# The first half of a gated feed-forward block: second-pair weight operands ahead of the second weight's, a gelu behind a copy, and another order of loads at the half's end

## The chip, the cores and the metric

The kernel runs on one core of a Trainium2 chip. The metric is device time in microseconds (us) of one execution. A core has five engines with an instruction queue each, and each queue is worked in order. TensorE (PE in the profile; PEld is its weight load) multiplies matrices into PSUM. VectorE (DVE) and ScalarE (ACT) work elementwise on PSUM and on-chip memory, GpSimd (POOL) elementwise on on-chip memory alone here. SyncE (SP) issues the DMA transfers. An instruction that waits for another engine's result holds up everything behind it on its own queue.

## The reference, cut to what matters

For 2048 tokens with 576 features, all in float32:

```
xn  = layernorm(x)
s   = linear attention of xn over 32 heads, times wo
h   = gelu_tanh(xn @ w1 + b1)          # w1: 576 x 4608
g   = silu(h @ w2 + b2)                # w2: 4608 x 576
out = x + s * g
```

## The kernel before

**Precision.** Each float32 operand is kept as two parts, a rounded high part and the rest (tiles named `_h` and `_l`, or one tile with both). A product is three matmuls: high by high, high by low, low by high. ACT makes the high part by a cast (line 811 for w1, 754 for w2 and h), DVE the low part by a subtraction (816 and 757). Both read the raw tile, and the low part waits for the high one.

**Stages.** The first 282.6 us make the attention part, and the layernormed x. Then the feed-forward runs over the tokens in two halves of 1024, and in each half over nine *chunks* of 512 of the 4608 hidden features, 18 chunks in all. This text counts them 0 to 17.

**Seven products for eight.** Each matrix product of a chunk is a 2 by 2 block product done with seven block products and sums of blocks (Winograd's variant of Strassen's scheme). A chunk has two *pairs* of feature blocks. For each pair the class `Up` does products M1, M2, M6, M5, M7, M3, M4, in this order, seven matmuls of 512 columns each. M1, M6 and M7 add up in the PSUM tile `a`, M5 and M3 in `e`; M2 and M4 go to the two halves of `bc`. So M6 may start only when ACT has copied M1 out of `a` (line 1107), M7 only when ACT has copied `a` again (`u1_sb`, line 1114), and M3 only when `e` has been copied (`m5_sb`, line 1117). DVE adds these copies to later products (lines 1110, 1120, 1125, 1129), and ACT takes four gelus of the sums (1098). A prime marks the second pair here: M5' is its product 5.

Then the *down product* multiplies the gelus by w2: `product` at line 1233, again seven block products in the order 1, 2, 7, 4, 5, 3, 6, each in two parts of twelve matmuls of 288 columns. Products 2, 4 and 3 add onto the PSUM tiles of 1, 7 and 5, after DVE has added what stood there to the sums `macc` (1239, 1243).

**Operands.** M1 and M2 take the w1 tile `wa`, M6 `w6`, M5 and M4 `wd`, M7 and M3 `wc`. In the first half the kernel makes these tiles itself: POOL makes the differences in place in the raw tile (`T`, lines 800 to 807), then ACT and DVE split them (`hi`, `lo`). They also go to DRAM, and the second half loads them from there. The same is done with w2's seven operands (`W2`, POOL line 1151). The first pair's w1 tiles are made during the chunk before (table `P0`), the second pair's during the first pair's products (table `P1`), w2's about the same time (table `PW2`).

**What sets the order.** Each of these tasks has a step number in a table. A chunk has 28 steps: 0 to 6 stand behind the first pair's products, 7 to 13 behind the second pair's, 14 to 27 behind the halves of the down product's parts. `at_step` writes out what is due after that product's own instructions. DVE, ACT, POOL and PE keep exactly the order in which the code writes instructions.

**The change of halves.** During chunk 8 the other half's x operands are loaded (`load_x_part`, line 1396, and `rxm` by `load_rests`): `h0`, `l0`, `h1`, `l1`, `s1`, `s2`, `s4` and `rxm` with 1 MB each, and three small pieces. Each goes over a tile of the first half, so it can start only after that tile's last product in chunk 8. `X_AT` holds their steps. Three finished output blocks (`C22`, `C21`, `C12`, parts of `macc`) get their silu (line 1309) in chunk 9, and are stored; later parts of the down product write over them.

Of the kernel before, what the change touches and what calls it, by code (L numbers as in the profile page):

```python
# [44 lines left out]
def linear_attention_gated_ffn(ctx, tc, x, xT, wqkv, wo, w1, w1e, b1, w2, b2, out):  # L45
# [733 lines left out]
    class W1:  # L779
# [11 lines left out]

        def T(self, i):

# [130 lines left out]
    def load_rests(half):  # L924

        if not rx:
            rx.append(xp.tile([P, KT, 512], F32R, tag="xh1", name="rxm"))
        t = rx[0]
        load_rest(half, REST_AT[1], 4, t[:, :4].rearrange("p k c -> p (k c)"))
        return {i: t[:, REST_AT[i] - REST_AT[1]] for i in (1, 7, 5, 3)}  # L930
# [25 lines left out]
    def beside(i, k):  # L956
# [14 lines left out]
        else:  # L971
# [24 lines left out]
            if i == 17:  # L996
                w = w1t[0]
                w.hi("a"), w.lo("a")
                for j in (5, 6, 7, 4):
                    w.T(j)  # L1000
                w.hi(6), w.lo(6)
# [9 lines left out]
    for i in range(1, NT + 4):  # L1011
        if 1 < i < NT:
            query(i)
        if i in X_STORES:
            at, src = X_STORES[i]
# [47 lines left out]
    C11, C12, C21, C22, U1 = range(5)  # L1063
# [8 lines left out]
    class Up:  # L1072
# [28 lines left out]
        def step(self, i):  # L1101
            A, E, Z = self.a, self.e, self.z[:, 0, :]
            B, C = self.bc[:, 0, :], self.bc[:, 1, :]
            tt = nc.vector.tensor_tensor
            if i == 1:
                self.mm(A, 1)
                nc.scalar.copy(m1_sb, A)  # L1107
            elif i == 2:
                self.mm(B, 2)
                tt(B, B, m1_sb, op=ADD)  # L1110
                self.gelu(0, 0, B)
            elif i == 6:
                self.mm(A, 6, first=False)
                nc.scalar.copy(u1_sb, A)
            elif i == 5:
                self.mm(E, 5)
                nc.scalar.copy(m5_sb, E)
            elif i == 7:
                self.mm(A, 7, first=False)
                tt(Z, A, m5_sb, op=ADD)  # L1120
                nc.scalar.copy(u2_sb, A)  # L1121
                self.gelu(1, 1, Z)
            elif i == 4:
                self.mm(C, 4)
                tt(C, C, u2_sb, op=ADD)
                self.gelu(0, 1, C)
            else:
                self.mm(E, 3, first=False)
                tt(E, E, u1_sb, op=ADD)  # L1129
                self.gelu(1, 0, E)  # L1130


    class W2:
# [9 lines left out]

        def T(self, i):
            src = self.src
# [26 lines left out]
    class HOps:  # L1172
# [6 lines left out]
        def add(self, pr, g):  # L1179
            for (par, b), t in g.items():  # L1180
                self.A[pr, b, par] = t
                self.src[{(0, 0): 1, (0, 1): 2, (1, 1): 4, (1, 0): "-"}[b, par], pr] = t
# [204 lines left out]
        "s2": (16, x_hi, 2, 6), "s1": (20, x_lo, 0, None), "h1": (8, x_hi, 3, 4),  # L1387
        "l1": (12, x_lo, 3, None),
    }
    X_AT = {"h0": 8, "l0": 11, "s2": 11, "h1": 13, "l1": 13, "s1": 13, "s4": 14}  # L1390
    x_new = {}

    def load_x_part(k):
# [10 lines left out]

    def plan_w1(add, w, base, T, hi, lo):
        for table, what in ((T, w.T), (hi, w.hi), (lo, w.lo)):
            for i, at in table.items():
                add(base + at, what, i)

    P1 = dict(  # L1410
        T={5: 1, 6: 1, 7: 3, 4: 3},
        hi={"a": 0, 6: 4, "c": 7, "d": 7},
        lo={"a": 0, 6: 5, "c": 8, "d": 8},
    )
    P0 = dict(
        T={5: 18, 6: 18, 7: 19, 4: 19},
        hi={"a": 16, 6: 23, "c": 25, "d": 27},
        lo={"a": 17, 6: 24, "c": 26, "d": 28},
# [1 line left out]


    PW2 = dict(
        T={5: -1, 7: 2, 6: 2, 4: 4},
        hi={1: -2, 3: -1, 2: 0, 5: 2, 7: 5, 6: 6, 4: 9},
        lo={1: -1, 3: 0, 2: 1, 5: 3, 7: 6, 6: 7, 4: 10},
    )

    def plan_w2(n, ahead):
        for what in ("hi", "lo", "T"):
# [7 lines left out]
        hi={  # L1437
            (1, 0): 7, (2, 0): 9, (7, 0): 10, (1, 1): 11, (2, 1): 12, (7, 1): 15, (4, 0): 16,
            (4, 1): 17, (5, 1): 18, (5, 0): 19, (6, 0): 20, (3, 0): 21, (3, 1): 22, (6, 1): 23,
        },  # L1440
        lo={
            (1, 0): 10, (2, 0): 10, (7, 0): 11, (1, 1): 12, (2, 1): 13, (7, 1): 15, (4, 0): 16,
            (4, 1): 17, (5, 1): 18, (5, 0): 19, (6, 0): 20, (3, 0): 21, (3, 1): 22, (6, 1): 23,
        },
# [17 lines left out]
    s2, s1, s4 = z.tiles  # L1462
# [4 lines left out]
    for step in range(n_chunks):  # L1467
        half, c = divmod(step, NC)
        base = step * NS
        plain = step == n_chunks - 1  # L1470
        h = HOps(c)
        if half == 0:
            plan_w1(add, w1t[2 * step + 1], base, **P1)
            if step == 0:
                plan_w2(0, True)
            plan_w2(step, False)
        change = step == NC - 1
        if not plain:
            add(base + (11 if change else 7), load_we, 2 * step + 2)
            add(base + (16 if change else 14), load_we, 2 * step + 3)  # L1480
        if half == 0 and c < NC - 1:
            add(base + 0, make, W1, w1t, 2 * step + 2)
            add(base + 4, make, W1, w1t, 2 * step + 3)
            add(base + 1, lambda n=2 * step + 2, base=base: plan_w1(add, w1t[n], base, **P0))
            make(W2, w2t, step + 1)
            add(base + 16, w2t[step + 1].load_raw)
            plan_w2(step + 1, True)
        elif not plain:
            add(base + (11 if change else 7), make, W1Loaded, w1t, 2 * step + 2)
            add(base + (11 if change else 14), load_six, 2 * step + 2)  # L1490
            add(base + (16 if change else 14), make, W1Loaded, w1t, 2 * step + 3)
            if step + 2 < n_chunks:
                make(W2, w2t, step + 1)
                for i, at in W2_NEXT.items():
                    add(base + at + 10 * change, lambda i=i, n=step + 1: w2t[n].load(i))
            else:
                make(W2, w2t, step + 1)

                w = w2t[step + 1]
                add(base + 7, w.load_raw)  # L1500
                for f in range(CF):
                    add(base + 22 + f, lambda f=f, w=w: (w.plain(f), w.hi(("p", f))))
                    add(base + 24 + f, w.lo, ("p", f))
        if not plain:
            if half == 0 and c == NC - 1:
                for k, at in X_AT.items():
                    add(base + at, load_x_part, k)
                add(base + 14, lambda: x_new.update(rs=load_rests(0)))
                add(base + 25, silu_first, C11)
                for k in range(2):  # L1510
                    add(base + 26 + k, combine, C12, nc.vector, slice(2 * k, 2 * k + 2))
                    add(base + 26 + k, combine, C21, nc.gpsimd, slice(2 * k, 2 * k + 2))
            for what in ("S", "hi", "lo"):
                for (i, pr), at in PH[what].items():
                    add(base + at, getattr(h, what), i, pr)
        if half == 1 and c == 0:
            add(base, combine, C22, nc.vector, slice(0, 2))
            add(base + 1, combine, C22, nc.vector, slice(2, 4))
            for m in (C22, C21, C12):
                add(base + 13, silu_first, m)  # L1520
        if half == 1 and c:
            for k in range(2):
                tiles = {}
                def load(k=k, t=7 + c, tiles=tiles):
                    tiles[0] = finish_tiles(k)
                    finish_load(t, k, tiles[0])
                add(base, load)
                add(base + 4, lambda k=k, t=7 + c, tiles=tiles: finish(t, k, tiles[0]))
        if plain:
            for m in (C12, C21, C22):  # L1530
                add(base + 4, combine, m, nc.gpsimd)
            for t, at in enumerate((6, 7, 12, 13, 5, 12, 12, 12)):
                add(base + at, load_xs, t)
            for b, f, at, lo in (
                (0, 0, 7, 8), (0, 1, 8, 9), (1, 0, 10, 10), (1, 1, 10, 11), (0, 2, 11, 12),
                (0, 3, 12, 13), (1, 3, 13, 13), (1, 2, 13, 13),
            ):
                add(base + at, tail_split, b, f)
                add(base + lo, tail_lo, b, f)
        for j in range(CF // 2):  # L1540
            n = 2 * step + j
            u = Up(n, w1t.pop(n), xs)
            for k, i in enumerate(UP):
                u.step(i)
                h.add(j, u.g)
                at_step(base + 7 * j + k)
        if plain:
            break
        held = {}
        for k, i in enumerate(ORDER):  # L1550
            for q2 in (0, 2):
                product(c, i, q2, [h.ops[i, 0], h.ops[i, 1]], w2t[step].ops[i], held)
                at_step(base + 14 + 2 * k + q2 // 2)
        if half == 0 and c == NC - 1:
            xs = x_operands(*(x_new[k] for k in ("h0", "l0", "h1", "l1", "s1", "s2", "s4", "rs")))
# [50 lines left out]
```

## Time and profile before

| what | value |
|---|---|
| time, median of 3 runs | 1113.93 us (1113.92 to 1115.60) |
| the profiled execution's own time | 1114.99 us |
| its span | 1113.3 us |
| DMA, mean over the span | 218 GB/s |
| chunks 0 to 8 | 282.61 to 700.48 us |
| chunks 9 to 17 | 700.48 to about 1105 us |

The page's first part gives each engine's busy time. The view of waits sums for an engine the idle time that ended when another engine's instruction was done: us in total, times, longest. The timeline has the start and length of each instruction. The view by stretches gives each stretch's length and what each engine was busy in it. Matmuls overlap, so a group's clean pitch is the time from one start to the next.

### The profile page before, as it was taken

Reading aid. Unit: us, or ns where it says so; the run is one execution under the profiler, and the core shown is the slowest. Engines: PE = TensorE matmul, PEld = TensorE weight load, DVE = VectorE, ACT = ScalarE, POOL = GpSimd, SP = SyncE. Lnnn points to the kernel's source line nnn. Section 1 sums busy time; section 2 is a strip of 40 time slices with the busy share of each in tenths; the row PEclk is TensorE's granted clock in tenths of the full one; section 3 lists DMA queues with packets and bytes.
Section 4 is the critical chain, followed back from the end, with each engine's and each line's share of the span. In section 5 each row is a group of like instructions: output and inputs, shape, how many; then the busy total and the mean of one; then the engine's idle time right before and its main releaser. Section 6 shows DMA issues by size and latency. Waiting matters only on the chain.

```text
span 1113.3 us, 18079 instructions
## 1 busy us (share of the span) xinstructions
PE 1095.2 (98%) x6702; PEld 1007.4 (90%) x6702; DVE 773.9 (70%) x1096; ACT 547.8 (49%) x954; POOL 455.7 (41%) x394
## 2 busy tenths in 40 slices
PE   9999999999999999999999999999999999999998
PEld 8999989999798888988889889898998998989988
DVE  7655338888688887888878888565474664754756
ACT  6444455454646455464554645445344253353552
POOL 3443214232647555475554754315133233241340
PEclk9999999999999999999999999999999999999999
DMA  6755124675759467485674829988667667766452
GB/s 212 216 137 143 58 76 161 205 255 178 272 238 331 188 226 257 186 327 191 224 260 187 324 114 377 379 310 280 215 221 229 221 219 235 221 221 209 146 187 87
DMA packets 84224, 242.78 MB, mean 218 GB/s; under 512 B 11430, under 2 KB 23718, under 8 KB 81448
## 3 DMA queue, kind: packets, MB, share of 16 engines
q1 hardware_dynamic: 84136, 241.62, 63.3%
q8 instruction: 53, 0.87, 0.3%
q14 instruction: 35, 0.29, 0.1%
HBM read 145.66 MB, written 93.99 MB: 215 GB/s over the span
## 4 chain that ended last, share of the span: by engine, by line
PE 87%; ACT 4%; DVE 3%; DMA 3%; issue 2%; SPq 0%; POOL 0%; ACTq 0%; DVEq 0%; POOLq 0%
PE pm L1233 32%; PE a L1090 11%; PE e L1090 8%; PE bc L1090 7%; PE pk L320 6%; PE pq L320 5%; PE ps_s L730 5%; PE pv L320 4%; PE pd L1349 2%; DMA rxm<-rq_dram 1%; PE ps_kva L381 1%; DVE wc L816 1%; DMA we<-op 1%; PE ptp L712 1%; DVE wd L816 1%
## 5 line engine op out<-in xcount | busy, mean ns | idle before, releaser
L1239 DVE TENSOR_TENSOR macc<-pm,macc 128x576 f32<-128x576 f32 x218 | 164.7, 756 | 63.4 <-PE pm L1233 61.4
L754 ACT CAST h_h<-g 128x512 fp32r<-128x512 f32 x204 | 121.8, 621 | 139.1 <-PE pm L1233 138.6
L757 DVE TENSOR_TENSOR h_l<-g,h_h 128x512 fp32r<-128x512 f32 x204 | 158.5, 780 | 12.1 <-ACT h_h L754 11.4
L1151 POOL TENSOR_TENSOR w2raw<-w2raw 128x576 f32<-128x576 f32 x36 | 60.7, 1687 | 99.6 <-DVE w__5651 L757 11.5
L1199 POOL TENSOR_TENSOR mid<-g 128x512 f32<-128x512 f32 x34 | 45.7, 1345 | 116.1 <-ACT g L1098 116.1
L1098 ACT ACTIVATE g<-bc,b1c 128x512 f32<-128x512 f32 x72 | 49.6, 689 | 54.7 <-DVE bc L1110 41.2
L1107 ACT COPY mid<-a 128x512 f32<-128x512 f32 x36 | 21.2, 588 | 96.9 <-PE a L1090 96.0
L1193 POOL TENSOR_TENSOR g<-g 128x512 f32<-128x512 f32 x34 | 51.9, 1526 | 31.1 <-DVE h_l L757 29.8
L1120 DVE TENSOR_TENSOR z<-a,mid 128x512 f32<-128x512 f32 x36 | 25.2, 700 | 56.4 <-PE a L1090 56.4
L1321 POOL TENSOR_TENSOR fin1l<-fin1h,fin1l 128x288 f32<-128x288 f32 x8 | 6.7, 837 | 120.7 <-DMA fin1l<-s_dram 69.9
L1110 DVE TENSOR_TENSOR bc<-bc,mid 128x512 f32<-128x512 f32 x36 | 25.0, 693 | 42.6 <-PE bc L1090 40.7
L1196 POOL TENSOR_TENSOR g<-g 128x512 f32<-128x512 f32 x34 | 49.2, 1448 | 7.6 <-DVE h_l L757 5.5
L1190 POOL TENSOR_TENSOR g<-g 128x512 f32<-128x512 f32 x34 | 47.5, 1397 | 2.7
L1121 ACT COPY mid<-a 128x512 f32<-128x512 f32 x36 | 21.1, 587 | 52.8 <-DVE z L1120 52.8
L695 POOL TENSOR_TENSOR pbuf<-phiq,den 128x576 f32<-128x576 f32 x16 | 19.4, 1212 | 63.6 <-DVE den L694 63.6
L320 PE MATMUL pk<-wkv_h,xh 128*128 128x288 f32 (+1 forms) x160 | 38.2, 321 | 0.4 <-ACT xh L247 0.4
L339 DVE SCALAR_TENSOR_TENSOR phik<-pk,ek 128x576 f32<-128x576 f32 x16 | 12.1, 758 | 38.2 <-ACT ek L337 38.2
L320 PE MATMUL pk<-wkv_l,xh 128*128 128x288 f32 (+1 forms) x160 | 38.2, 321 | 0.0
L1090 PE MATMUL e<-s,wd 128*128 128x512 f32 x108 | 30.0, 400 | 7.8 <-DVE wd L816 7.8
L1129 DVE TENSOR_TENSOR e<-e,mid 128x512 f32<-128x512 f32 x36 | 25.1, 696 | 16.8 <-PE e L1090 16.8
L730 PE MATMUL ps_s<-kw_h,th 128*128 128x288 f32 x160 | 35.5, 303 | 0.0
L320 PE MATMUL pq<-wq_h,xh 128*128 128x288 f32 x160 | 34.8, 299 | 0.0
(894 smaller groups left out, 3638.6 us busy)
## 6 DMA issues: line engine op xcount, KB each, us to landing
we<-we_dram SPq DMA_DIRECT2D x36, 448.0 KB
w2raw<-w SPq DMA_DIRECT2D x10, 1152.0 KB
w1raw<-w SPq DMA_DIRECT2D x18, 512.0 KB
op_a<-wa SPq DMA_DIRECT2D x18, 512.0 KB
op_c<-wc SPq DMA_DIRECT2D x18, 512.0 KB
op_d<-wd SPq DMA_DIRECT2D x18, 512.0 KB
wc<-op_c SPq DMA_DIRECT2D x18, 512.0 KB
wa<-op_a SPq DMA_DIRECT2D x18, 512.0 KB
```

The source lines that it names most:

```text
L320: nc.tensor.matmul(ps[:, h, : ws.stop - ws.start], st, w[:, k, ws], start=(begin and i == 0), stop=(end and i == len(seq) - 1), skip_group ...
L730: nc.tensor.matmul(ps[:, h, :HD], st[:, k, :], w[:, k, h * HD : (h + 1) * HD], start=(i == 0), stop=(i == len(seq) - 1),)
L754: nc.scalar.copy(pair[0], src)
L757: eng.tensor_tensor(pair[1], src, pair[0].bitcast(F32), op=SUB)
L1090: nc.tensor.matmul(ps, st, mv, start=first and n == 0, stop=n == len(seq) - 1, skip_group_check=True,)
L1098: nc.scalar.activation(g, ps, AF.Gelu_apprx_tanh, bias=b1c[:, f : f + 1])
L1151: tt(dst, a, b, op=SUB)
L1190: tt(src[5, pr], A(1, 0), A(1, 1), op=ADD)
L1193: tt(src[6, pr], src[5, pr], A(0, 0), op=SUB)
L1196: tt(src[3, pr], A(0, 1), src[6, pr], op=SUB)
L1233: nc.tensor.matmul(ps[:, q, :HD], hs[p][st][:, cs], m[:, p, :], start=(n == 0 and i not in CHAIN), stop=(n == 5), skip_group_check=True,)
L1239: nc.vector.tensor_tensor(dst, src, dst, op=ADD)
```

## The change

- In the first half's chunks the tasks of the tables move. The second pair's `wc` and `wd` are made at steps 5 and 6 in place of 7 and 8, and POOL's two sums for them at step 2 in place of 3. w2's operands for products 7, 6 and 4 come one or two steps later, the low parts for 3 and 2 and POOL's sums for 7 and 6 one step later.
- In `Up`, for all chunks, the gelu of M2's sum is written after the copy of `a` behind M6, and no longer ahead of it.
- At the change of halves the loads of x come in another order and at other steps; `load_rests` (`rxm`) goes from step 14 to 12.
- The three silus of chunk 9 are due at steps 13, 15 and 18; before, all were due at step 13.

```diff
@@ Up.step
             elif i == 2:
                 self.mm(B, 2)
                 tt(B, B, m1_sb, op=ADD)
-                self.gelu(0, 0, B)
             elif i == 6:
                 self.mm(A, 6, first=False)
                 nc.scalar.copy(u1_sb, A)
+                self.gelu(0, 0, B)
@@ loads of x
-    X_AT = {"h0": 8, "l0": 11, "s2": 11, "h1": 13, "l1": 13, "s1": 13, "s4": 14}
+    X_AT = {"l0": 8, "s2": 8, "h0": 9, "s1": 12, "h1": 13, "l1": 13, "s4": 14}
...
-                add(base + 14, lambda: x_new.update(rs=load_rests(0)))
+                add(base + 12, lambda: x_new.update(rs=load_rests(0)))
@@ P1
-        T={5: 1, 6: 1, 7: 3, 4: 3},
-        hi={"a": 0, 6: 4, "c": 7, "d": 7},
-        lo={"a": 0, 6: 5, "c": 8, "d": 8},
+        T={5: 1, 6: 1, 7: 2, 4: 2},
+        hi={"a": 0, 6: 4, "c": 5, "d": 5},
+        lo={"a": 0, 6: 5, "c": 6, "d": 6},
@@ PW2
-        hi={1: -2, 3: -1, 2: 0, 5: 2, 7: 5, 6: 6, 4: 9},
+        hi={1: -2, 3: -1, 2: 0, 5: 2, 7: 6, 6: 8, 4: 10},
...
@@ silus
-            for m in (C22, C21, C12):
-                add(base + 13, silu_first, m)
+            for m, at in ((C22, 13), (C21, 15), (C12, 18)):
+                add(base + at, silu_first, m)
```

The instruction order on DVE in chunk 3, from its second pair's `wa` on, stood as follows. Here `bc6`, `z6` and `e6` are the first pair's sums and `bc7` the second's; `wc_7` and `wd_7` are the second pair's w1 tiles; the tiles `w2_3` are w2's, of which this queue makes the low parts.

```order
L816 TENSOR_TENSOR wa_7_4711<-w1raw7_4287,wa_7_4711 128x512
L757 TENSOR_TENSOR w2_3__4688<-w2raw3_4483,w2_3__4688 128x576
L1110 TENSOR_TENSOR bc6_4698<-bc6_4698,mid_3217 128x512
L757 TENSOR_TENSOR w2_3__4716<-w2raw3_4483,w2_3__4716 128x576
...
L816 TENSOR_TENSOR w6_7_4775<-w1t6_4734,w6_7_4775 128x256
L1125 TENSOR_TENSOR bc6_4698<-bc6_4698,mid_3217 128x512
L757 TENSOR_TENSOR w2_3__4793<-w2raw3_4483,w2_3__4793 128x576
L757 TENSOR_TENSOR w2_3__4805<-w2raw3_4483,w2_3__4805 128x576
L1110 TENSOR_TENSOR bc7_4812<-bc7_4812,mid_3217 128x512
L816 TENSOR_TENSOR wc_7_4822<-w1raw7_4287,wc_7_4822 128x512
L816 TENSOR_TENSOR wd_7_4824<-w1raw7_4287,wd_7_4824 128x512
L757 TENSOR_TENSOR w2_3__4860<-w2raw3_4483,w2_3__4860 128x576
```

In the changed kernel it is this:

```order
L816 TENSOR_TENSOR wa_7_4711<-w1raw7_4287,wa_7_4711 128x512
L1110 TENSOR_TENSOR bc6_4698<-bc6_4698,mid_3217 128x512
L757 TENSOR_TENSOR w2_3__4688<-w2raw3_4483,w2_3__4688 128x576
...
L816 TENSOR_TENSOR w6_7_4775<-w1t6_4729,w6_7_4775 128x256
L1125 TENSOR_TENSOR bc6_4698<-bc6_4698,mid_3217 128x512
L816 TENSOR_TENSOR wc_7_4790<-w1raw7_4287,wc_7_4790 128x512
L816 TENSOR_TENSOR wd_7_4792<-w1raw7_4287,wd_7_4792 128x512
L757 TENSOR_TENSOR w2_3__4813<-w2raw3_4483,w2_3__4813 128x576
L1110 TENSOR_TENSOR bc7_4817<-bc7_4817,mid_3217 128x512
L757 TENSOR_TENSOR w2_3__4844<-w2raw3_4483,w2_3__4844 128x576
...
L1120 TENSOR_TENSOR z7_4818<-a7_4815,mid_3217 128x512
```

The low parts of `wc_7` and `wd_7` moved ahead of two w2 tiles and of the second pair's first sum; the last w2 tile went behind `z7`.

On ACT at the start of chunk 3, before, behind the copy of M1 (`a6` is the first pair's tile `a`, `e6` its `e`):

```order
L754 CAST w2_3__4716<-w2raw3_4483 128x576
L1098 ACTIVATE g_4731<-bc6_4698,b1c_78 128x512
L1114 COPY mid_3217<-a6_4696 128x512
L754 CAST w2_3__4747<-w2raw3_4483 128x576
L1117 COPY mid_3217<-e6_4697 128x512
```

In the changed kernel:

```order
L754 CAST w2_3__4716<-w2raw3_4483 128x576
L1113 COPY mid_3217<-a6_4696 128x512
L1098 ACTIVATE g_4742<-bc6_4698,b1c_78 128x512
L754 CAST w2_3__4746<-w2raw3_4483 128x576
L1117 COPY mid_3217<-e6_4697 128x512
```

The copy of `a` and the gelu changed places. Where ACT must load a function table for the gelu, in chunks 0, 9 and 10, that load now stands between the copy and the gelu.

On SP in chunk 8, the loads at the change of halves, before (`l0r` to `s4r` are the x tiles; `we`, `wa` and `wd` are w1's for chunk 9):

```order
L1396 DMA l0r<-x_dram 128x2048
L751 DMA op_c<-wc_7263 128x1024
L751 DMA op_d<-wd_7265 128x1024
L1396 DMA h0r<-x_dram 128x2048
...
L1396 DMA s2r<-x_dram 128x2048
L920 DMA s2r<-rq_dram 128x512
L1396 DMA h1r<-x_dram 128x2048
L920 DMA h1r<-rq_dram 128x512
L1396 DMA l1r<-x_dram 128x2048
L1396 DMA s1r<-x_dram 128x2048
L1396 DMA s4r<-x_dram 128x2048
L920 DMA rxm<-rq_dram 128x2048
```

In the changed kernel:

```order
L751 DMA op_d<-wd_7235 128x1024
L1396 DMA l0r<-x_dram 128x2048
L1396 DMA s2r<-x_dram 128x2048
L920 DMA s2r<-rq_dram 128x512
L1396 DMA h0r<-x_dram 128x2048
...
L1396 DMA s1r<-x_dram 128x2048
L920 DMA rxm<-rq_dram 128x2048
L1396 DMA h1r<-x_dram 128x2048
L920 DMA h1r<-rq_dram 128x512
L1396 DMA l1r<-x_dram 128x2048
L1396 DMA s4r<-x_dram 128x2048
```

The load of `rxm` went from the last place to before `h1r`, `l1r` and `s4r`, and `s2r` went ahead of `h0r`.

More of the change, by code (lines that the diff above doesn't have):

```diff
@@ L1422, in linear_attention_gated_ffn @@
     PW2 = dict(
-        T={5: -1, 7: 2, 6: 2, 4: 4},
-        hi={1: -2, 3: -1, 2: 0, 5: 2, 7: 5, 6: 6, 4: 9},
-        lo={1: -1, 3: 0, 2: 1, 5: 3, 7: 6, 6: 7, 4: 10},
+        T={5: -1, 7: 3, 6: 3, 4: 4},
+        hi={1: -2, 3: -1, 2: 0, 5: 2, 7: 6, 6: 8, 4: 10},
+        lo={1: -1, 3: 1, 2: 2, 5: 3, 7: 7, 6: 9, 4: 11},
     )
```

## The prediction

> **What bounds the kernel now.** I read the page's busy times first, then the engines' waits, the stretches, and the timeline of one chunk. The page:
>
> ```profile
> PE 1095.2 (98%) x6702; PEld 1007.4 (90%) x6702; DVE 773.9 (70%) x1096; ACT 547.8 (49%) x954; POOL 455.7 (41%) x394
> ```
>
> PE works nearly all the time, so only its pauses can be won. The waits of its weight loads and matmuls name them:
>
> ```profile
> PEld e L1090 <- DVE wd L816: 11.6, 9, 2.2
> PEld a L1090 <- ACT mid L1114: 4.8, 9, 1.1
> PE a L1090 <- DMA rxm<-rq_dram: 1.1, 1, 1.1
> PE pm L1233 <- ACT h_h L754: 0.5, 1, 0.5
> PE pm L1233 <- DVE h_l L757: 0.4, 1, 0.4
> ```
>
> Two waits come once in each of the nine first-half chunks: for the low part of `wd`, and for the copy of `a`. What a chunk loses is in the stretches of chunks 0, 3, 8, 9 and 10 (length, then busy times, granted clock, DMA share, GB/s):
>
> ```profile
> 282.61:330.48 47.87, 45.44 (x269) 40.65 (x268) 37.84 (x49) 28.33 (x49) 26.41 (x20) 1.00 0.67 256
> 423.07:469.34 46.27, 45.47 (x269) 40.66 (x268) 38.72 (x51) 25.17 (x45) 25.91 (x20) 1.00 0.64 237
> 654.44:700.48 46.04, 45.24 (x269) 40.64 (x268) 37.36 (x49) 24.50 (x41) 22.81 (x17) 1.00 0.84 321
> 700.48:747.96 47.48, 45.48 (x269) 40.79 (x268) 28.82 (x40) 23.43 (x35) 13.65 (x10) 1.00 0.91 345
> 747.96:792.60 44.64, 44.64 (x268) 40.79 (x267) 25.85 (x36) 19.08 (x31) 14.68 (x13) 1.00 0.76 258
> ```
>
> All chunks do the same matmuls at the same clock. In chunk 10 PE never pauses: 44.64 us is a chunk without waits. Against it chunk 0 loses 3.23, chunks 1 to 7 (330.48 to 654.44, 46.28 each) 1.64 each, chunk 8 1.40 and chunk 9 2.84: 18.9 in all, the most that this change can bring. DVE is busy for 38.7 of 46.3 us in the first half, so its order matters there. Chunk 3 on PE:
>
> ```profile
> 427.88 1.52 PE L1090 MATMUL e<-s,wd 128*128 128x512 f32 x6
> 429.24 0.39 PE L1090 MATMUL e<-rxm,we 128*128 128x512 f32 x1
> 430.01 0.39 PE L1090 MATMUL a<-xl,wc 128*128 128x512 f32 x1
> ...
> 439.33 0.61 PE L1090 MATMUL e<-s,wd 128*128 128x512 f32 x2
> 440.70 1.19 PE L1090 MATMUL e<-s,wd 128*128 128x512 f32 x4 [0.76 <-DVE wd L816]
> 441.74 0.40 PE L1090 MATMUL e<-rxm,we 128*128 128x512 f32 x1
> 446.73 0.42 PE L1233 MATMUL pm<-w__4669,h_h 128*128 128x288 f32 x2
> ...
> 455.92 0.43 PE L1233 MATMUL pm<-w__4793,h_h 128*128 128x288 f32 x2
> 456.18 0.29 PE L1233 MATMUL pm<-w__4793,h_l 128*128 128x288 f32 x1
> 456.47 0.50 PE L1233 MATMUL pm<-w__4860,h_h 128*128 128x288 f32 x2
> 456.81 0.30 PE L1233 MATMUL pm<-w__4860,h_l 128*128 128x288 f32 x1
> ```
>
> M5's six matmuls take 1.36 us (427.88 to 429.24), a pitch of 0.227. M5' takes 2.41: `wd` costs **1.05**. From 429.24 to 430.01 two matmuls take 0.77 and not 0.45: the copy costs **0.32**. From 456.18 to 456.81 three take 0.63; at the pitch before (0.26 for two) it would be 0.39: **0.24**, where down product 4 waits for DVE to empty product 7's PSUM. The sum, 1.61, is the stretch's loss.
>
> **The change part by part.** Times are now counted from the chunk's first matmul (423.07), with PE unbroken at 1.59 a product: M6 ends at 4.8, M5 at 6.35, M7 at 7.95, M4 at 11.1; M5' meets the low part of `wd` at 16.3; the down product starts at 22.2.
>
> ```profile
> 427.74 0.69 DVE L1110 TENSOR_TENSOR bc<-bc,mid 128x512 f32<-128x512 f32 x1
> 446.31 0.68 DVE L757 TENSOR_TENSOR h_l<-g,h_h 128x512 fp32r<-128x512 f32 x1
> 428.46 0.69 ACT L1098 ACTIVATE g<-bc,b1c 128x512 f32<-128x512 f32 x1 [1.89 <-DVE bc L1110]
> 429.05 0.57 ACT L1114 COPY mid<-a 128x512 f32<-128x512 f32 x1
> ...
> L816 DVE TENSOR_TENSOR wc<-w1raw,wc x18: 681/934/1189, 280.2 to 670.2; 128x512 fp32r<-128x512 f32 x18
> L816 DVE TENSOR_TENSOR wd<-w1raw,wd x18: 676/684/1756, 280.9 to 671.3; 128x512 fp32r<-128x512 f32 x18
> L1151 POOL TENSOR_TENSOR w2raw<-w2raw 128x576 f32<-128x576 f32 x36 | 60.7, 1687 | 99.6 <-DVE w__5651 L757 11.5 <-DVE w__4178 L757 11.5 <-DVE w__6142 L757 11.5
> ```
>
> *`wc` and `wd` earlier.* They now follow M4's sum on DVE: M4 ends at 11.1, 0.2 to be seen, 0.7 for the sum, so 12.0. Two low parts take 1.4 at the shortest and 1.19 + 1.76 = 2.95 at the longest, so `wd` is there between 13.4 and 14.95, ahead of 16.3. ACT's two casts stand before the last gelu of the pair and wait for POOL's sums, which now come before two of w2's. The wait of 1.05 goes in each chunk, and chunk 0's of 2.1.
>
> *w2's operands later.* None is due before 22.2, the moved ones not before product 7 at 28.6, and POOL's three remaining w2 sums (3 x 1.69) end near 13. What pays is DVE behind the second pair: w2's last low part now stands between `z7` and the second pair's later sums and low parts. Product 1 takes the low part `h11` after ten matmuls, at 23.5. In the trace it ended at 446.99 (446.31 + 0.68), where the down product, begun at 446.73, met it 1.33 later: about 1.1 to spare. With one more low part (0.75 to 1.5) after `z7`, which can start at 19.25, four more operations of 0.65 to 1.2 follow: it ends between 22.6 and 23.9. So the cost is between 0 and 0.5 a chunk. I take 0, since most of the range lies under 23.5.
>
> *Product 4's wait* of 0.24 stays: the w1 low part for the next chunk still stands ahead of the sum that frees the PSUM. That low part takes 0.68 alone and up to 1.12 beside POOL, whose sums come somewhat later: 0 to 0.44 more. I take 0.1, near the lower end, for chunks 1 to 7: +0.7.
>
> *The gelu behind the copy.* M6 ends at 4.8; the copy runs from 5.0 to 5.55, before M7 at 6.35: 0.32 goes. Behind it now stand the gelu (0.6 to the next), a w2 cast (0.57) and the copy of `e`, which ends at 7.3; M3 needs it at 7.95. In chunks 0, 9 and 10 a table load stands there too:
>
> ```profile
> 286.55 0.67 ACT L754 CAST w__3243<-w2raw 128x576 fp32r<-128x576 f32 x1
> 287.24 1.28 ACT L1098 ACT_TABLE_LOAD   x1
> 288.54 0.69 ACT L1098 ACTIVATE g<-bc,b1c 128x512 f32<-128x512 f32 x1
> ```
>
> Before, it ran while ACT waited for M2's sum; that cover is gone. The copy of `e` ends at 5.55 + 1.28 + 0.6 + 0.6 = 8.0 in chunks 9 and 10 and, with the cast, 8.6 in chunk 0. With some 0.15 to start PE again, M3 waits **0.2** and **0.8** there.
>
> The Trainium skill ("ScalarE: Activation LUTs", What ACT_TABLE_LOAD costs) adds a drain of about 1380 ns to 1283 ns of load. Here the load starts 0.02 us after the cast's end and the gelu 0.02 after the load's, so no run here shows a drain; with one, the three waits would grow by 1.38 each.
>
> *The change of halves.*
>
> ```profile
> 686.72 0.32 SPq L920 DMA_DIRECT2D rxm<-rq_dram  x1
> 703.17 0.47 PE L1090 MATMUL a<-rxm,we 128*128 128x512 f32 x1 [1.14 <-DMA rxm<-rq_dram]
> 727.07 3.27 ACT L1309 ACTIVATE macc<-macc 128x1152 f32<-128x1152 f32 x3
> ```
>
> `rxm` was the last of eight 1 MB loads and took 16.4 us to land, behind the others in the queue; with the restart it costs 1.4. Now `s4r` is last. It is needed at M3, 6.6 us later in the chunk than `rxm`'s first use (7.95 against 1.36), where `rxm` was 1.4 late: some 5 us to spare, and the bytes are the same. So 1.4 goes. The three silus held up ACT for 3.27 us, and with it the casts of h: 1.2 in chunk 9. Now only one silu stands ahead of the first cast, and another ahead of the second; that goes too. The sum that writes over `C22` must wait for that block's store; it stands about 4 us behind the silu. That costs 0 to 1; I take 0, since nothing large is queued before the store.
>
> *The rest.* POOL's moved sums and SP's stores and weight loads in another order cost nothing: the stores are read in the next half, and the raw tiles a chunk later. If a store held up SP, the w1 load behind it would have 15 us before its use.
>
> **The sum**, against the profiled execution (span 1113.3, time 1114.99, 1.06 above the median):
>
> chunk 0: 3.23 less 0.8 and 0.24, that is -2.2; chunks 1 to 7: 7 x 1.37 = -9.6; chunk 8: -1.4; chunk 9: 2.84 less 0.2, that is -2.6; chunk 10: +0.2; product 4's wait: +0.7. Together -14.9: the span comes to 1098.4, and the median of the runs to 1113.93 - 14.9 = **1099.0 us**.
>
> **The rivals.**
>
> 1. *DVE becomes the bound behind the second pair.* For it: 38.7 us of work in 44.9, and a low part at up to 23.9 where 23.5 is the limit. Against it: DVE still has 6 us idle a chunk. At 0.5 a chunk, nine times: 1103.5.
> 2. *The wait for the copy moves on to M3* in all first-half chunks, if M2's sum comes late and holds gelu and copy of `e`. For it: the row at 428.46 above, where the gelu waited 1.89 us for that sum; against it: the sum now stands one w2 low part earlier on DVE. 0.32 x 8 = 2.6: 1101.6.
> 3. *The loads of x are hidden no better*, and `h1r` or `s4r` is late in place of `rxm` (0.91 DMA share in chunk 9): 1.4 comes back: 1100.4.
> 4. *A drain at the table loads*, 1.38 for each of three waits: 1103.1. Against it the 0.02 us gaps. (This is the page's rule above.)
> 5. *Slower: DVE and POOL shut each other out.* Both read operands from on-chip memory, and POOL's three w2 sums now run together beside `wc`'s and `wd`'s low parts. If each of these waited for a whole POOL sum, it would take 1.69 + 0.68 = 2.37: `w6`'s low part ends at 12.5, M4's sum 13.2, `wd` 17.9, and M5' waits 1.8; the next w2 low part and M2's sum (2.37 + 0.7) bring the copy of `e` behind the gelu to 22.7, against M3' at 19.05 + 1.8: 1.9 more. 3.7 a chunk in place of 1.37, nine times, less 2.4 for the rest: about 1132. It decides from the point where `wd` ends later than 17.7. Against it: the rows above have 0.93 and 0.68 as medians, with POOL as busy before.
>
> The Trainium skill ("SBUF — State Buffer", Who interferes with whom) says that a VectorE operation with two SBUF inputs and a GpSimd one that reads SBUF block each other fully; the trace has 0.68 to 1.76 us for one form, so some waiting, seldom a whole sum of 1.69.
>
> **How the numbers follow.** Forecast 0.73; rivals 0.13, 0.04, 0.05, 0.02 and 0.03. The forecast's own range is 1097 to 1101 (no growth of product 4's wait gives 1098.3; 0.44 a chunk 1101.4; all pauses gone would be 1095.0). To take in rival 1 the range is 1096.5 to 1103.5. This kernel's measurement tells 0.2%, about 2.2 us: all cases but the last are faster (0.95, some held back for what I overlooked); the same 0.02, slower 0.03.
>
> **What would show it.** In the profile after: no wait of PE for `wd`; the copy of `a` gone from the waits, and in its place waits of `e` for ACT, one of 0.8 and two of 0.2; chunks 1 to 7 at 44.9 to 45.0, chunk 8 at 44.65, chunk 9 at 44.9; no wait for `rxm`. The forecast is wrong if chunks 1 to 7 stay above 45.4: then a wait of `pm` for `h_l` or of `e` for `wd` says whether DVE is the bound.

## The result and the profile after

| what | before | changed |
|---|---|---|
| time, median | 1114.76 us (4 runs, 1113.92 to 1116.43) | 1122.14 us (4 runs, 1120.96 to 1122.74) |
| ratio | | 1.0063, 95% interval 1.0046 to 1.0080 |
| span of the profiled execution | 1113.3 us | 1120.1 us |

The kernel became slower by 0.6%, where a gain of 1.3% was forecast: 1122.1 us stand against a forecast of 1099.0, with a range of 1096.5 to 1103.5. The length of the chunks, from first matmul to first matmul, shows where:

| chunk | before | forecast | changed | difference to before |
|---|---|---|---|---|
| 0 | 47.87 | 45.7 | 47.34 | -0.5 |
| 1 to 7, each | 46.28 | 45.0 | 46.64 | +0.36, together +2.5 |
| 8 | 46.04 | 44.65 | 46.03 | 0 |
| 9 | 47.48 | 44.85 | 51.89 | +4.4 |
| 10 | 44.65 | 44.85 | 44.93 | +0.3 |

With 0.2 us in the attention part this is the span's growth of 6.8. The view by stretches for chunks 0, 3, 8, 9 and 10 of the changed kernel (length, then busy times of PE, PEld, DVE, ACT and POOL, granted clock, DMA share, GB/s):

```profile
282.84:330.18 47.34, 45.70 (x269) 40.78 (x268) 39.81 (x49) 28.24 (x49) 26.55 (x20) 1.00 0.68 259
423.43:470.06 46.63, 45.73 (x269) 40.78 (x268) 41.82 (x51) 25.08 (x45) 26.51 (x20) 1.00 0.63 236
656.60:702.64 46.04, 45.70 (x269) 40.78 (x268) 40.37 (x49) 24.41 (x41) 23.43 (x17) 1.00 0.84 325
702.64:754.53 51.89, 46.72 (x269) 42.06 (x267) 29.60 (x40) 23.18 (x35) 14.03 (x10) 0.97 0.84 311
754.53:799.46 44.93, 44.93 (x269) 40.71 (x268) 25.70 (x36) 18.82 (x31) 14.85 (x13) 1.00 0.77 260
```

The row to stop at is chunk 3's. DVE does the same 51 instructions, and is busy for 41.8 us where it was busy for 38.7. The same work takes 3.1 us longer.

**A steady chunk.** The waits of PE and of its weight loads in chunk 3, 423.43 to 470.06 (us in total, times, longest):

```profile
PE pm L1233 <- DVE macc L1239: 0.6, 1, 0.6
PEld pm L1233 <- ACT h_h L754: 0.8, 1, 0.8
PEld e L1090 <- ACT mid L1117: 0.6, 1, 0.6
PEld pm L1233 <- DVE h_l L757: 0.4, 1, 0.4
PEld pm L1233 <- DVE macc L1239: 0.3, 1, 0.3
```

No wait for `wd` is left, and none for the copy of `a`. Three others have come, and product 4's has grown: the first two rows are the same stop, product 4's, where DVE's sum was the last to come (PE's row). By the matmuls' starts against the clean pitch the second pair's M3 (M3') loses 0.41, product 1 loses 0.38 for a low part, product 2 loses 0.31, and product 4 loses 0.84 where it lost 0.24: 1.94 in all, where the two waits that went and product 4's were worth 1.61. All four come from DVE, M3' by way of ACT. The timeline of DVE's queue behind the first pair's last product, with POOL's ahead of it and ACT and PE behind (start, length):

```profile
431.92 4.52 POOL L1151 TENSOR_TENSOR w2raw<-w2raw 128x576 f32<-128x576 f32 x3
436.56 1.58 POOL L1199 TENSOR_TENSOR mid<-g 128x512 f32<-128x512 f32 x1
438.22 1.62 POOL L1190 TENSOR_TENSOR g<-g 128x512 f32<-128x512 f32 x1
...
435.07 0.69 DVE L1125 TENSOR_TENSOR bc<-bc,mid 128x512 f32<-128x512 f32 x1
435.67 1.33 DVE L816 TENSOR_TENSOR wc<-w1raw,wc 128x512 fp32r<-128x512 f32 x1
436.92 1.78 DVE L816 TENSOR_TENSOR wd<-w1raw,wd 128x512 fp32r<-128x512 f32 x1
438.62 1.85 DVE L757 TENSOR_TENSOR w__4813<-w2raw,w__4813 128x576 fp32r<-128x576 f32 x1
440.39 0.69 DVE L1110 TENSOR_TENSOR bc<-bc,mid 128x512 f32<-128x512 f32 x1
...
441.11 0.69 ACT L1098 ACTIVATE g<-bc,b1c 128x512 f32<-128x512 f32 x1 [0.95 <-DVE bc L1110]
441.69 0.61 ACT L754 CAST h_h<-g 128x512 fp32r<-128x512 f32 x1
442.20 0.59 ACT L1117 COPY mid<-e 128x512 f32<-128x512 f32 x1
...
442.85 1.66 PE L1090 MATMUL e<-s,wc 128*128 128x512 f32 x6
```

Three low parts stand between the first pair's last sum and the sum of M2', and take 1.33, 1.78 and 1.85 us beside POOL's sums. DVE has no idle time between them. So the sum of M2' starts 17.0 us into the chunk (440.39), where before it started at 15.2:

```profile
438.26 0.69 DVE L1110 TENSOR_TENSOR bc<-bc,mid 128x512 f32<-128x512 f32 x1
```

The gelu behind the copy waits for it, the copy of `e` waits behind the gelu, and M3' waits for that copy. DVE then stays behind until the down product. At product 4 it meets the next chunk's `wa`:

```profile
455.70 0.68 DVE L816 TENSOR_TENSOR wa<-w1raw,wa 128x512 fp32r<-128x512 f32 x1
456.30 0.74 DVE L1239 TENSOR_TENSOR macc<-pm,macc 128x576 f32<-128x576 f32 x1
457.19 0.50 PE L1233 MATMUL pm<-w__4871,h_h 128*128 128x288 f32 x2 [0.59 <-DVE macc L1239]
```

Before, that sum was this row, in a chunk that began at 423.07:

```profile
455.58 0.74 DVE L1239 TENSOR_TENSOR macc<-pm,macc 128x576 f32<-128x576 f32 x1
```

So it now starts 0.36 us later in the chunk (32.87 and 32.51), and PE comes there 0.24 earlier: together the 0.60 by which product 4's wait grew.

**Chunk 9.** SP's issues, the silu behind the second store, and what waits for that store:

```profile
729.30 0.55 SPq L1310 DMA_DIRECT2D c_dram<-macc  x1
729.95 0.58 SPq L773 DMA_DIRECT2D we<-we_dram  x1
...
733.21 0.43 SPq L840 DMA_DIRECT2D wd<-op_d  x1
733.74 0.41 SPq L1170 DMA_DIRECT2D w__7860<-op  x1
734.26 0.55 SPq L1310 DMA_DIRECT2D c_dram<-macc  x1
...
729.69 1.16 ACT L1309 ACTIVATE macc<-macc 128x1152 f32<-128x1152 f32 x1
...
744.30 0.76 DVE L1243 TENSOR_TENSOR macc<-pm,b2b 128x576 f32<-128x576 f32 x1 [7.32 <-DMA c_dram<-macc]
745.11 0.85 PE L1233 MATMUL pm<-w__7700,h_h 128*128 128x288 f32 x2 [4.87 <-DVE macc L1243]
```

Before, the three stores were issued together and chunk 10's loads behind them:

```profile
728.26 2.62 SPq L1310 DMA_DIRECT2D c_dram<-macc  x3
730.93 1.35 SPq L847 DMA_DIRECT2D we<-op  x1
```

Now only the first store (`C22`) is ahead. All w1 loads for chunk 10 and a w2 tile are issued between it and the second (`C21`). That silu had ended at 730.85 (729.69 and 1.16), the store was issued at 734.26, and it was done only at about 744.3, when DVE could write product 4's sum over `C21`'s block. This sum also empties a PSUM tile, and product 5's second part, which needs a tile, waits 4.87 for it.

### The profile page after: what moved, and what is told of

Read it like the earlier page. It is cut to its first block, busy times and chain, and to the rows that moved or that the text cites. A ratio compares the mean times of both kernels' runs of the same rounds, so it can differ in the third digit from the quotient of the medians.

```text
span 1120.1 us, 18080 instructions
## 1 busy us (share of the span) xinstructions
PE 1099.1 (98%) x6702; PEld 1009.6 (90%) x6702; DVE 802.0 (72%) x1096; ACT 544.8 (49%) x954; POOL 461.2 (41%) x394
## 4 chain that ended last, share of the span: by engine, by line
PE 78%; DVE 11%; ACT 4%; DMA 3%; issue 2%; POOL 1%; SPq 1%; DVEq 0%; ACTq 0%
PE pm L1233 26%; PE a L1090 12%; PE e L1090 7%; PE bc L1090 7%; PE pk L320 6%; PE pq L320 5%; PE pv L320 4%; PE ps_s L730 4%; DVE h_l L757 4%; PE pd L1349 2%; DVE macc L1239 1%; ACT h_h L754 1%; PE ps_kva L381 1%; ACT g L1098 1%; POOL mid L1199 1%
## 5 line engine op out<-in xcount | busy, mean ns | idle before, releaser
L1151 POOL TENSOR_TENSOR w2raw<-w2raw 128x576 f32<-128x576 f32 x36 | 55.5, 1542 | 100.4 <-DVE w__7124 L757 11.5
L1107 ACT COPY mid<-a 128x512 f32<-128x512 f32 x36 | 21.2, 588 | 95.6 <-PE a L1090 94.4
L1193 POOL TENSOR_TENSOR g<-g 128x512 f32<-128x512 f32 x34 | 52.7, 1550 | 29.5 <-DVE h_l L757 28.2
L1196 POOL TENSOR_TENSOR g<-g 128x512 f32<-128x512 f32 x34 | 53.2, 1565 | 10.8 <-DVE h_l L757 8.8
L1113 ACT COPY mid<-a 128x512 f32<-128x512 f32 x36 | 21.1, 587 | 62.0 <-PE a L1090 62.0
L1190 POOL TENSOR_TENSOR g<-g 128x512 f32<-128x512 f32 x34 | 47.0, 1383 | 2.7
L757 DVE TENSOR_TENSOR h_l<-mid,h_h 128x512 fp32r<-128x512 f32 x34 | 40.3, 1186 | 4.5 <-ACT h_h L754 4.5
L1121 ACT COPY mid<-a 128x512 f32<-128x512 f32 x36 | 21.2, 590 | 40.0 <-DVE z L1120 40.0
```

What stands on the lines that cost most here:

```text
L757: eng.tensor_tensor(pair[1], src, pair[0].bitcast(F32), op=SUB)
L1151: tt(dst, a, b, op=SUB)
L1193: tt(src[6, pr], src[5, pr], A(0, 0), op=SUB)
L1196: tt(src[3, pr], A(0, 1), src[6, pr], op=SUB)
```

## The experiments

### Each part alone

The tables alone (`P1` and `PW2`):

```diff
-        hi={"a": 0, 6: 4, "c": 7, "d": 7},
-        lo={"a": 0, 6: 5, "c": 8, "d": 8},
+        hi={"a": 0, 6: 4, "c": 5, "d": 5},
+        lo={"a": 0, 6: 5, "c": 6, "d": 6},
...
-        lo={1: -1, 3: 0, 2: 1, 5: 3, 7: 6, 6: 7, 4: 10},
+        lo={1: -1, 3: 1, 2: 2, 5: 3, 7: 7, 6: 9, 4: 11},
```

> The kernel before with the tables alone (second-pair tiles early, the second weight's operands late; gelu, loads of x and silus as before). Theory 1 (the tables are what costs in the steady chunks: DVE is late behind the second pair): the wait for wd of 1.05 us a chunk is gone, but the second pair's first gelu waits until 17.7 us into the chunk for its sum, and with the gelu ahead of the copy the second pair's product 7 waits about 1.4 us for that copy. Chunks 1 to 7 at 47.3 to 48.3 us against 46.28 before, span 1121 to 1130. Rival (the tables gain and the gelu behind the copy costs): chunks 1 to 7 at or below 45.6, span at or below 1108.

Measured: span 1127.5, ratio 1.0130 (1.0115 to 1.0145), most of the chunks 1 to 7 at 48.08. Theory 1 holds, and the rival falls. The chain is the expected one: the gelu stands ahead of the copy, waits for the late sum, and holds the second pair's product 7 for 1.8 us (about 1.4 was expected).

```profile
445.40 0.69 ACT L1098 ACTIVATE g<-bc,b1c 128x512 f32<-128x512 f32 x1 [3.05 <-DVE bc L1110]
446.54 0.59 ACT L1114 COPY mid<-a 128x512 f32<-128x512 f32 x1
447.18 0.50 PE L1090 MATMUL a<-xh,wc 128*128 128x512 f32 x1 [1.78 <-ACT mid L1114]
```

So the gelu behind the copy is what keeps the new tables from costing 14 us; with it they cost 0.36 a chunk.

The gelu behind the copy alone:

```diff
                 tt(B, B, m1_sb, op=ADD)
-                self.gelu(0, 0, B)
...
                 nc.scalar.copy(u1_sb, A)
+                self.gelu(0, 0, B)
```

> The kernel before with the gelu behind the copy alone. Theory 1: the copy's wait (0.32 a chunk, 0.95 in chunk 0) goes and nothing comes in its place in chunks 1 to 8; the table load costs 0.8 in chunk 0, 0.25 each in chunks 9 and 10, as in the changed kernel. Chunks 1 to 7 at 45.95, span about 1111. Rival (the gelu behind the copy makes product 3 wait by itself, 0.41 as in the changed kernel's second pair): chunks 1 to 7 at 46.3 to 46.4, span 1113.5 to 1114.5.

Measured: span 1117.1, ratio 1.0012 (1.0003 to 1.0022), chunks 1 to 7 at 46.50. Neither theory. Product 3 waits in chunks 0, 9 and 10 alone, so the rival's mechanism is not there; but the 0.32 is not won either. The row of waits shows who took it (before: 11.6):

```profile
PEld e L1090 <- DVE wd L816: 14.4, 9, 2.3
...
442.27 0.68 DVE L816 TENSOR_TENSOR wd<-w1raw,wd 128x512 fp32r<-128x512 f32 x1
```

The same low part in the kernel before:

```profile
439.97 0.68 DVE L816 TENSOR_TENSOR wd<-w1raw,wd 128x512 fp32r<-128x512 f32 x1
```

It starts 16.88 us into the chunk that begins at 425.39, and before at 439.97 - 423.07 = 16.90. DVE's queue is not paced by PE there, so when PE comes 0.32 earlier it waits 0.32 longer for `wd`. Product 4's wait grew as well, from 0.15 to 0.40 at its first matmul; no run shows by what. Chunk 0 took 49.6 in place of 47.9, with a lower clock behind the wait for `wd` (last section).

The loads of x alone:

```diff
-    X_AT = {"h0": 8, "l0": 11, "s2": 11, "h1": 13, "l1": 13, "s1": 13, "s4": 14}
+    X_AT = {"l0": 8, "s2": 8, "h0": 9, "s1": 12, "h1": 13, "l1": 13, "s4": 14}
...
-                add(base + 14, lambda: x_new.update(rs=load_rests(0)))
+                add(base + 12, lambda: x_new.update(rs=load_rests(0)))
```

> The kernel before with the loads of x in the new order alone. Theory 1: chunk 9 loses its wait for rxm (1.3 us), nothing else: chunk 9 at 46.2, span 1112.0. Rival (another x tile comes late in its place): chunk 9 at 47.0 to 47.5, span 1113.0 to 1113.5.

Measured: chunk 9 at 46.10, span 1111.8; the time's ratio of 0.9992 (0.9983 to 1.0002) can't tell it from none. The wait for `rxm` is gone, and no other tile is late. Theory 1 holds: 1.38 us.

The silus alone:

```diff
-            for m in (C22, C21, C12):
-                add(base + 13, silu_first, m)
+            for m, at in ((C22, 13), (C21, 15), (C12, 18)):
+                add(base + at, silu_first, m)
```

> The kernel before with the silus spread over steps 13, 15 and 18 alone. Theory 1 (the second and third stores now stand behind chunk 10's w1 loads in SP's queue, and the sum that writes over C21 waits for the store): chunk 9 grows by 3.5 to 5 us to 51 to 52.5, DVE waits about 7 us for the store, span 1117 to 1118.5. Rival (the store was late only because the loads of x come in another order): chunk 9 shrinks by up to 1.2 to 46.3, span 1112.

Measured: chunk 9 at 50.41, 2.9 longer than before, span 1117.8, ratio 1.0035 (1.0022 to 1.0048). The wait is there without the new order of loads, so the rival falls:

```profile
742.61 0.76 DVE L1243 TENSOR_TENSOR macc<-pm,b2b 128x576 f32<-128x576 f32 x1 [5.29 <-DMA c_dram<-macc]
```

Chunk 9 and the wait are shorter than expected (5.29 where the changed kernel has 7.32): here PE is still held up by `rxm` at the chunk's start and DVE comes 0.9 later in the chunk to that place, and the store is done 1.1 earlier in it. Of the span's growth, 1.6 lies in chunk 0, which this edit doesn't touch (last section).

The changed kernel without the silus' spread (all three at step 13 again):

> The changed kernel with the three silus back at step 13. Theory (the store behind chunk 10's loads cost chunk 9 about 5 us): chunk 9 at 46.1 to 46.5 in place of 51.89, chunks 1 to 7 unchanged at 46.64, span 1114.3 to 1114.9. Rival (part of chunk 9's growth comes from the other parts): chunk 9 at 47.5 or more, span above 1115.7.

Measured: chunk 9 at 46.36, chunks 1 to 7 at 46.62, span 1113.9 (a little below what was expected), ratio 1.0012 (1.0003 to 1.0021). So the spread cost 5.5 us in the changed kernel: the whole growth of chunk 9, and what the loads had won there. The next two runs start from this kernel.

### Why DVE is late

POOL's sums of w2's blocks and of the gelus cut to 32 columns; the rest of each sum is left out (two of the five places shown):

```diff
-            tt(dst, a, b, op=SUB)
+            tt(dst[..., :32], a[..., :32], b[..., :32], op=SUB)
...
-                tt(src[5, pr], A(1, 0), A(1, 1), op=ADD)
+                tt(src[5, pr][:, :32], A(1, 0)[:, :32], A(1, 1)[:, :32], op=ADD)
```

> The kernel of f0_nosilus with POOL's sums of w2's blocks and of the gelus over 32 columns in place of 512 or 576 (the sums of the rest are left out, and product 7's operand is a gelu itself, so the output isn't the reference's); the order on every engine is the same. Theory (DVE's low parts take up to 1.85 us because POOL reads and writes the same on-chip memory): the low parts of wd and of the w2 tile behind it fall from 1.78 and 1.85 to 0.7 to 0.8, DVE's busy time of a chunk from 41.8 to 36 or less, the waits of product 3 and of the down product go, chunks 1 to 7 at 44.65 to 45.0. Rival (the order on DVE alone makes it late): the low parts shrink but chunks 1 to 7 stay above 45.9.

Measured: 1098.77 us in one run, span 1097.1. Chunks 1 to 8 take 44.65 us, the length without any wait. The stretch of chunk 3 and the row of the `wd` low parts (shortest, median, longest in ns), then the same row of the changed kernel:

```profile
417.44:462.08 44.64, 44.64 (x268) 40.79 (x267) 34.88 (x51) 25.03 (x45) 12.43 (x20) 1.00 0.66 246
...
L816 DVE TENSOR_TENSOR wd<-w1raw,wd x18: 683/684/693, 281.0 to 653.2; 128x512 fp32r<-128x512 f32 x18
...
L816 DVE TENSOR_TENSOR wd<-w1raw,wd x18: 684/1236/1915, 281.1 to 670.1; 128x512 fp32r<-128x512 f32 x18
```

DVE's order is the same as in f0_nosilus, its 51 instructions now take 34.9 us in place of 41.8, and all four waits are gone, product 4's with them. The order alone does not make DVE late; the order in which POOL's sums run beside its low parts does.

The sum of M2' ahead of one w2 low part:

```diff
-        lo={1: -1, 3: 1, 2: 2, 5: 3, 7: 7, 6: 9, 4: 11},
+        lo={1: -1, 3: 1, 2: 2, 5: 3, 7: 8, 6: 9, 4: 11},
```

> The kernel of f0_nosilus with DVE's sum of the second pair's M2 written ahead of one w2 low part (product 7's) and not behind it. Theory: only product 3's wait for the copy of e (0.41) hangs on that sum, and the down product's waits hang on how much DVE has to do in all, so they take over what product 3 gives back: chunks 1 to 7 at 46.4 to 46.65, span 1113.0 to 1114.8. Rival (the waits add up, each by itself): chunks 1 to 7 at 46.2, span 1111.5.

Measured: chunks 1 to 7 at 46.00, span 1109.3, ratio 0.9965 (0.9953 to 0.9978). The theory is wrong, and the rival nearer but short: M3' no longer waits, which by itself would give 46.2, and product 1's wait fell too, from 0.38 to 0.20. DVE's busy time fell from 41.8 to 40.7. That low part alone takes 1.25 in place of 1.85, since it now starts nearer to the end of POOL's sum: how long DVE is busy is itself a matter of the order.

```profile
421.98:467.96 45.98, 45.35 (x268) 40.88 (x267) 40.73 (x51) 25.13 (x45) 26.45 (x20) 1.00 0.63 239
```

### What the change was after, in another way

The kernel before, with the new order of the loads and one exchange: `wd` against w2's tile for product 6.

```diff
-        hi={"a": 0, 6: 4, "c": 7, "d": 7},
-        lo={"a": 0, 6: 5, "c": 8, "d": 8},
+        hi={"a": 0, 6: 4, "c": 7, "d": 6},
+        lo={"a": 0, 6: 5, "c": 8, "d": 7},
...
-        hi={1: -2, 3: -1, 2: 0, 5: 2, 7: 5, 6: 6, 4: 9},
-        lo={1: -1, 3: 0, 2: 1, 5: 3, 7: 6, 6: 7, 4: 10},
+        hi={1: -2, 3: -1, 2: 0, 5: 2, 7: 5, 6: 7, 4: 9},
+        lo={1: -1, 3: 0, 2: 1, 5: 3, 7: 6, 6: 8, 4: 10},
```

> The kernel before with the new order of the loads of x, and on DVE and ACT one exchange in each first-half chunk: the second pair's wd tile takes the place of w2's tile for product 6 (in front of the sum of M2), which is made behind wc. No more is asked of DVE ahead of the second pair's sums than before. Theory: the wait for wd (1.05) goes and nothing comes in its place, since DVE had 1.1 us to spare ahead of z: chunks 1 to 7 at 45.2 to 45.35, chunk 0 at 45.8 to 46.8, chunk 9 at 46.1, span 1102 to 1104.5. Rival (DVE is the bound and the wait turns up at the down product): chunks 1 to 7 at 46.0 or above, span 1110 or above.

Measured: 1105.01 us, ratio 0.9913 (0.9898 to 0.9928), span 1103.4, chunks 1 to 7 at 45.33 (one of them 45.50), chunk 0 at 46.78, chunk 9 at 46.10. The theory holds, but not to the last tenth: 0.1 of the 1.05 comes back at product 4, whose wait grew from 0.24 to 0.35, and the one chunk at 45.50 lies above the expected 45.35. The stretch of chunk 3 has DVE at 38.74 us, as in the kernel before:

```profile
420.26:465.59 45.33, 45.17 (x268) 40.73 (x267) 38.74 (x51) 25.18 (x45) 26.16 (x20) 1.00 0.64 242
```

Then the low part of the next chunk's `wa` behind the sum that empties product 7's PSUM (POOL's sums in its raw tile one step later):

```diff
-        T={5: 18, 6: 18, 7: 19, 4: 19},
+        T={5: 19, 6: 19, 7: 20, 4: 20},
...
-        lo={"a": 17, 6: 24, "c": 26, "d": 28},
+        lo={"a": 18, 6: 24, "c": 26, "d": 28},
```

> The kernel of g1_swap with DVE's low part of the next chunk's wa written behind the sum that empties product 7's PSUM and no longer ahead of it (step 18 in place of 17; POOL's sums in that raw tile follow one step later, at 19 and 20). Theory: product 4's wait (0.27 us in chunks 1 to 7, 1.03 in chunk 0) is that low part of 0.68 in the queue ahead of the sum, so it goes: chunks 1 to 7 at 45.05 to 45.1, span 1100.4 to 1101.4. Rival (the next chunk's w6 and wc become late with POOL's later sums, or the next sum on DVE does): chunks 1 to 7 at 45.3 or above, span 1103 or above.

Measured: 1102.00 us, ratio 0.9888 (0.9874 to 0.9903), span 1100.8, chunks 1 to 7 at 44.99 (one 45.12). As expected, and 0.06 to 0.1 better.

Then the gelu behind the copy, where neither a table load nor a late sum stands in the way:

```diff
+            self.late = n % 2 == 0 and 2 <= n < 2 * NC
...
                 tt(B, B, m1_sb, op=ADD)
-                self.gelu(0, 0, B)
+                if not self.late:
+                    self.gelu(0, 0, B)
...
                 nc.scalar.copy(u1_sb, A)
+                if self.late:
+                    self.gelu(0, 0, B)
```

> The kernel of g2_wa with the first gelu behind the copy of a in the first pairs of chunks 1 to 8 alone (no table load stands there, and the second pairs keep the old order). Theory (the wait for the copy, 0.32 a chunk, could not be won in e2_gelu since the late wd took it over; with wd early it can): chunks 1 to 7 at 44.7 to 44.85, span 1098 to 1099. Rival (DVE takes it over at another place, as in e2_gelu): chunks 1 to 7 at 45.0 to 45.1, span 1100.5 or above.

Measured: 1101.14 us, ratio 0.9881 (0.9866 to 0.9895), span 1099.4, chunks 1 to 7 at 44.91. Between the two: the copy's wait of 0.32 is gone, 0.24 of it has come back at product 4, and 0.08 is won. Again DVE took most of what PE gained; chunk 8 reaches 44.69.

Last, two silus at step 13 and `C12`'s behind the first cast, with chunk 10's loads behind all three stores:

```diff
-            for m in (C22, C21, C12):
-                add(base + 13, silu_first, m)
+            for m, at in ((C22, 13), (C21, 13), (C12, 15)):
+                add(base + at, silu_first, m)
...
-            add(base + (16 if change else 14), load_we, 2 * step + 3)
+            add(base + (16 if change or step == NC else 14), load_we, 2 * step + 3)
...
```

> The kernel of g3_gelu with the silu of C12 at step 15, behind the first cast of a gelu, and with chunk 10's loads of w1 and of w2's first tile two steps later, so that all three stores stay ahead of them in SP's queue. Theory: product 7's wait in chunk 9 (0.57) goes and product 4's (0.61) stays, no sum waits for a store: chunk 9 at 45.5, span 0.5 to 0.7 below g3_gelu. Rival (chunk 10's tiles become late): chunk 10 above 45, span not below g3_gelu.

Measured: 1100.48 us (1100.11 to 1100.77), ratio 0.9875 (0.9859 to 0.9892), span 1098.4. Chunk 9 lost product 7's wait and a little more, and chunk 10 is at its clean length: the theory holds, with 0.83 in place of 0.57, and the span is 1.0 lower where 0.5 to 0.7 was expected.

```profile
418.59:463.49 44.90, 44.90 (x269) 40.83 (x267) 39.80 (x51) 25.08 (x45) 26.37 (x20) 1.00 0.64 245
687.82:733.09 45.27, 44.88 (x269) 40.80 (x267) 28.79 (x40) 23.31 (x35) 14.13 (x10) 1.00 0.89 339
733.09:777.74 44.65, 44.65 (x269) 40.78 (x268) 25.86 (x36) 19.07 (x31) 14.86 (x13) 1.00 0.81 286
```

This version is faster than both kernels: 14 us below the one before, 22 below the change.

## Why the prediction was wrong

**Right.** What bounds the kernel (PE's pauses), the size of the pauses, and that the waits for `wd` and for the copy would go: both are gone. The table loads behind the copy cost what was forecast: M3 waits 0.82 in chunk 0 (0.8) and 0.25 in chunks 9 and 10 (0.2). The loads of x gave 1.38 (1.4). Product 4's wait stayed, as forecast; its size is step 2.

**Wrong, step 1: "What pays is DVE behind the second pair ... I take 0".** It measured 1.10 a chunk (M3' 0.41, product 1 0.38, product 2 0.31). Two things failed in it. It worked out one deadline, product 1's, and left out M3' (product 2's wait for a sum is not in it either): the gelu behind the copy was followed through the first pair alone (copy of `e` at 7.3, needed at 7.95), though in the second pair the three moved low parts stand ahead of the sum that this gelu waits for. And it gave the low parts 0.75 to 1.5 each, the lengths they had at their old places; at the new ones they ran beside POOL's sums and took up to 1.85. For product 1 it had the low part ready 22.6 to 23.9 us into the chunk; it was ready at 24.27 (447.70 - 423.43). The sum `z7` ahead of it started 0.27 later than worked out, and one low part took 1.78 where 1.2 was the longest in the sum. The length of an instruction was carried along as if it belonged to the instruction.

**Wrong, step 2: product 4's wait, "0 to 0.44 more. I take 0.1".** It grew by 0.60 (0.84 against 0.24). The cause named was the right one, the `wa` low part in the queue ahead of the sum; the run with that low part moved shows it. What was missed is that the sum comes 0.36 later in the chunk, though that `wa` low part takes its 0.68 as before, and that PE comes 0.24 earlier.

**Wrong, step 3: the silus, "I take 0, since nothing large is queued before the store".** It measured 5.5 us in chunk 9. The order on SP in that chunk was not read. The prediction looked at `C22`'s store, which stayed the first; chunk 10's loads were due at step 14, so `C21`'s, of step 15, stood behind all of them. This one step is most of the difference to the kernel before.

Of the 21.7 us between the forecast span (1098.4) and the measured one, step 1 makes about 9.9 in chunks 0 to 8, step 2 about 4.3, and chunk 9 7.0, with step 3's 5.5 in it.

**Adding up waits.** The sum took each wait as worth its length. The gelu alone shows that it need not be so: `wd` came when DVE's queue brought it, and 0.32 won ahead of it was lost at it. With POOL's sums short nothing is lost again: chunks 1 to 8 take 44.65, and product 4's wait, which the prediction kept in its 45.0 for chunks 1 to 7, is gone too.

**The rivals.** Rival 5 named the mechanism, DVE and POOL shutting each other out, and rivals 1 and 2 two of the places where it showed. Rival 5's price of 3.7 a chunk was too high because it gave every low part a whole POOL sum to wait for. Measured is the rest of the POOL sum that is running when the low part starts: `wd`'s started at 436.92, POOL's sum ended at 438.14 (436.56 and 1.58), and 0.68 more makes 438.82, where 438.70 was measured; the next one started at 438.62, POOL's ended at 439.84, and with 0.75 that makes 440.59, where 440.47 was measured. The rule of the Trainium skill ("SBUF — State Buffer", Who interferes with whom), that a VectorE operation with two inputs in on-chip memory and a GpSimd one that reads it block each other fully, agrees with these rows. The prediction's reading of the spread ("some waiting, seldom a whole sum") was not false, but it put no price on it; the rows above price it.

## What to carry to other kernels

Where two engines shut each other out, an instruction's length belongs to the place in which it runs: before moving it, look at what the other engine does there, and price it by the rest of that. A wait of the engine that bounds the kernel (PE here) is won only as far as the queue that feeds the next wait is not already behind. And a store whose buffer is soon written over must be read in the order of its DMA queue, with every load that is issued ahead of it.

## What was not expected of the hardware

**POOL holds up low parts, but not sums that read PSUM.** In chunks 1 to 7 of the changed kernel 85 low parts started while a POOL sum had over 0.3 us to go. They took 1.35 us on average (0.91 to 1.85), and each of the 85 took the rest of that POOL sum and its own undisturbed length (0.68, 0.75 or 0.42 by shape), less 0.13 to 0.14. The 91 that started with POOL idle took 0.67 on average, and the 21 of these beside which a POOL sum then began were no longer for it (0.69 at most). The sums of a PSUM tile with a copy took 0.69 in either case: the row at 435.07 above runs inside POOL's 4.52 us. The Trainium skill ("SBUF — State Buffer", Who interferes with whom) says this of VectorE operations with at most one input in on-chip memory, and the trace agrees.

**After a wait of about 2 us the clock may fall.** In chunk 0 the second pair waits 2.1 us for `wd`, in the kernel before and, with the same instructions, in e4_silus. The 2 us from 302 on, first before, then in e4_silus (granted clock third from the end):

```profile
302.00:304.00 2.00, 2.00 (x9) 1.63 (x10) 1.65 (x3) 0.65 (x2) 0.78 (x1) 1.00 0.68 78
```

```profile
302.00:304.00 2.00, 2.00 (x6) 1.59 (x5) 1.51 (x3) 0.03 (x1) 0.92 (x1) 0.53 0.65 80
```

In the second the matmuls ran at a pitch of 0.43 in place of 0.227 us until about 305.5, and the chunk took 1.64 us longer. The same is seen in e2_gelu's chunk 0, in e1_tables after one of the waits of 1.8 us that each of its chunks 1 to 7 has (0.50 from 449 to 451), and in the changed kernel's chunk 9 after its 4.87 us, where it makes some 1.3 of step 3's 5.5. So a wait near 2 us can cost nearly twice its length, in some executions and not in others. The Trainium skill ("TensorE: Matmul & The Clock Gate", Part 1) has the clock fall after an idle window of about 3.4 us; but for the 4.87 us of chunk 9, these rows have it after less, so the measured 1.8 to 2.2 us count here. The 20 runs of the kernel before in one comparison lie 3.0 us apart and the four of g1_swap 0.24; the clock would fit that, but no run here tests it.
